# 29 of w_o's 32 blocks summed by row groups in place of 28

## The chip, the core and the metric

The kernel runs on one core of one Trainium2 chip. The metric is the device time of one execution in microseconds, the median over runs. The engines are named as in the profile: PE is TensorE's matmul (PEld its weight loads), DVE VectorE, ACT ScalarE, POOL GpSimd, SP the engine that issues most transfers. Times in a view of the trace are counted from the start of the span, the first instruction of the profiled execution.

## The reference

```python
x = A_x                                   # [2, 1, 512], float32 like everything here
xn = layernorm(x)
q = xn @ wq                               # 32 heads of 128
scores = q . k_cache[last 4096 rows] * 128 ** -0.5     # 8 kv heads, 4 query heads each
o = softmax(scores) . v_cache[last 4096 rows]
s = o.reshape(2, 1, 32 * 128) @ wo        # wo is [4096, 512]
z = gelu(xn @ w_in)                       # [2, 1, 1792]
g = (z1 * (w_sp * layernorm(z2) + b_sp)) @ w_out
out = x + s * silu(g)
```

Some 89 MB are read for two rows of output: 2 x 8 x 4096 x 128 values of each cache, wq (512 x 4096), wo (4096 x 512) and the two weights of the gate.

## The kernel before

Everything large passes through `ring`, four slots of 4 MB in the on-chip memory. `enqueue` and `advance` (lines 85 to 99) hand out the slots in order: SP issues a load as soon as its slots are free. The order of loads is w_in, w_out, wq, then the K and V windows of eight units (one unit is one batch row and two kv heads), and last w_o in three pieces of 16, 8 and 8 blocks.

A block of w_o is a [128, 512] matrix: `wo_v` (line 161) puts row p * 32 + j of w_o in partition p of block j, so s is the sum over 32 blocks of a [128, 2] piece of the attention's output times the block. `load_blocks` (164 to 180) issues one transfer for the first 16 blocks, one for the next 8, and for the last piece `(4, 1, 1, 1, 1)`: one of 1 MB for blocks 24 to 27 and one of 256 KB each for 28, 29, 30 and 31. They come over in that order, and w_o's last block is the last thing that the kernel reads.

Every engine works in program order (`InOrder`, line 27). The loop over units (469 to 497) turns K on DVE, multiplies on TensorE, copies on ACT; 498 to 511 finish the last two units. `collect` (444) multiplies a unit's heads by `sel` into 32 columns of the tile `col`, `gather` (454) makes of that `oT` (line 465), in which `oT[:, n, :]` is block n's left operand: 32 columns of 128 partitions, of which columns 0 and 16 hold the two batch rows.

TensorE's array is used in four column groups of 32 here: a product whose left operand has 32 columns writes 32 rows of the output tile, and four products for different rows (`part[32 * g : 32 * g + 32]`) can run side by side, one in each group. The last projection uses this in two ways.

*By row groups* (516 to 519): block n is multiplied in its full width of 512 columns, into rows of group n % 4 of the tile `part`. Each group sums every fourth block. Afterwards ACT copies `part` to `parts` (521), and `spread_quarters` (310 to 314) multiplies each column quarter of `parts` by `rowm`, which adds the four groups and puts quarter g of the result into rows of group g of the tile `so`. This is called the spread here.

*By column quarters* (523 to 531): block n's 512 columns are cut into four quarters of 128, and quarter g goes straight into rows of group g of `so`, four products per block, with no copy behind them.

`EARLY` is the number of blocks that go by row groups, and the others go by quarters. `LATE` = 30 says ahead of which block of the loop the spread is issued. Before the change: row groups for blocks 0 to 27, ACT's copy, quarters of 28 and 29, the spread, quarters of 30 and 31. All of `so` is one accumulation; DVE then multiplies by the gate (533), adds x (534), and SP stores the result (535).

Every product in this kernel is of float32 values and stands in the trace as two instructions (two passes), each with a weight load of its own.

Of the kernel before, what the change touches and what calls it, by code (L numbers as in the profile page):

```python
# [42 lines left out]
def kernel(  # L43
# [60 lines left out]
    def bank(name, tag):  # L104
        return ps.tile([P, 512], F32, tag=tag, name=name, bufs=BANKS[tag])
# [405 lines left out]
    gather(last)  # L511


    EARLY, LATE = 28, 30
    part = bank("part", "sh")
    for n in range(EARLY):
        t, a = blocks[n]
# [46 lines left out]
```

## Time and profile before

| what | us |
|---|---|
| median of 3 runs (217.80 to 218.05) | 217.91 |
| the profiled execution | 217.37 |
| its span, first to last instruction | 215.6 |
| busy: PE / DVE / ACT | 156.5 / 107.5 / 44.0 |
| HBM read | 89.40 MB, 415 GB/s over the span |
| ACT's copy of `part` | 0.60 |
| products of blocks by row groups, 56 instructions | 7.9 |

The page gives busy time by engine, the span in 40 slices (tenths of each slice, 9 is 90% or more), and the chain of work that ended last, by engine. A row of the timeline has its start and length, the engine, the operation, output and inputs, and a count; like instructions that follow each other are merged, and in brackets stands how long the engine was idle before and what ended that. All rows carry line 37, where the helper `InOrder` issues them, so that one tells instructions apart by their tiles: `part` (row groups), `so` from `ring` (quarters), `so` from `parts` (the spread), `col` (collecting heads). Ends of matmuls are modelled, starts are recorded.

### The profile page before, as it was taken

What the parts mean: (1) busy time and instruction counts of PE and PEld (TensorE: products, weight loads), DVE (VectorE), ACT (ScalarE), POOL (GpSimd) and SP (SyncE); (2) the same over time, 40 slices, a digit from 0 to 9 for tenths busy, and PEclk for the clock granted to TensorE, in tenths of its full rate; (3) what the DMA queues carried; (4) which work ended last, traced back from release to release, by engine and by line L of the source; (5) the groups of instructions that cost most, each with busy time, mean ns of one, the idle gap of its engine ahead of it and who ended that gap; (6) DMA issues with size and microseconds to landing.
All of it is one profiled execution on the core that took longest, in us unless ns stands there. A gap on an engine that the chain in (4) does not pass through costs nothing.

```text
span 215.6 us, 2230 instructions
## 1 busy us (share of the span) xinstructions
PE 156.5 (73%) x866; PEld 43.6 (20%) x866; DVE 107.5 (50%) x168; ACT 44.0 (20%) x109; POOL 3.9 (2%) x21
## 2 busy tenths in 40 slices
PE   0164273952994995995997699559959948999793
PEld 0121110210121221221221222222212212222321
DVE  3304313058968647837906941695587089240101
ACT  5002410000223143133113304120431421232001
POOL 6100000000000000000000000000000000000000
PEclk9999567695598899799699679958997995899799
DMA  7999898999999999999999999999999999999991
GB/s 251 426 528 401 389 499 371 423 444 409 456 407 450 426 435 432 426 438 413 450 412 438 432 438 435 432 432 407 432 444 423 444 426 450 413 441 413 404 388 40
DMA packets 3789, 89.54 MB, mean 415 GB/s; under 512 B 434, under 2 KB 450, under 8 KB 964
## 3 DMA queue, kind: packets, MB, share of 16 engines
q1 hardware_dynamic: 3772, 89.40, 97.0%
q8 instruction: 7, 0.11, 0.2%
q14 instruction: 2, 0.02, 0.0%
q10 hardware_dynamic: 8, 0.00, 0.0%
HBM read 89.40 MB, written 0.00 MB: 415 GB/s over the span
## 4 chain that ended last, share of the span: by engine, by line
DMA 48%; PE 34%; DVE 15%; issue 1%; SPq 0%; DVEq 0%
DMA ring<-in_A_wo_dram 20%; DMA ring<-in_A_wq_dram 16%; DMA ring<-in_A_k_cache_dram 12%; DVE kt L37 10%; PE s L37 10%; PE sh L37 9%; PE acc L37 7%; PE q_ps L37 4%; PE col L37 1%; PE mo L37 1%; DVE qm L37 1%; DVE qbd L37 1%; DVE m L37 1%; PE rp L37 1%; PE oT L37 0%
## 5 line engine op out<-in xcount | busy, mean ns | idle before, releaser
L37 DVE STREAM_TRANSPOSE kt<-ring 128x2048 f32<-128x2048 f32 x32 | 72.6, 2294 | 32.5 <-DMA ring<-in_A_k_cache_dram 30.5
L37 PE MATMUL sh<-kt,qbd 128*32 128x512 f32 x256 | 43.4, 727 | 14.0 <-DVE kt L37 14.0
L37 ACT ACTIVATE shs<-sh 128x512 f32<-128x512 f32 x32 | 19.1, 597 | 119.1 <-PE sh L37 119.1
L37 PE MATMUL s<-shs,add_dq 128*128 128x512 f32 x64 | 41.0, 748 | 0.0
L37 PE MATMUL acc<-ring,pT 128*32 128x512 f32 x256 | 30.3, 612 | 0.2 <-DVE pT L37 0.2
L37 PEld LDWEIGHTS s<-shs,add_dq 128*128 128x128 f32 x64 | 11.2, 219 | 31.1 <-issue 26.7
L37 PEld LDWEIGHTS sh<-kt,qbd 128*32 128x32 f32 x256 | 6.7, 114 | 34.2 <-issue 20.4
L37 PEld LDWEIGHTS acc<-ring,pT 128*32 128x32 f32 x256 | 7.4, 114 | 24.7 <-issue 15.5
L37 PE MATMUL q_ps<-ring,xnT 128*32 128x512 f32 x64 | 9.6, 770 | 3.6 <-DMA ring<-in_A_wq_dram 3.6
L37 PE MATMUL mo<-l,same_r 128*128 128x2 f32 x16 | 3.7, 299 | 10.7 <-ACT p L37 10.7
L37 DVE TENSOR_REDUCE m<-s 128x2 f32<-128x512 f32 x8 | 5.4, 675 | 9.1 <-PE s L37 9.1
L37 ACT ACTIVATE o<-acc,wd 128x128 f32<-128x128 f32 x32 | 9.1, 373 | 3.4 <-PE acc L37 3.4
L37 PE MATMUL z<-ring,xnT 128*32 128x448 f32 x32 | 5.6, 875 | 5.3 <-DMA ring<-in_B_w_in_dram 5.3
L37 ACT ACTIVATE p<-s,nb 128x256 f32<-128x256 f32 x16 | 7.6, 490 | 7.0 <-DVE nb L37 6.8
L37 PE MATMUL part<-ring,oT 128*32 128x512 f32 x56 | 7.9, 714 | 1.1 <-DMA ring<-in_A_wo_dram 1.1
L37 PE MATMUL col<-o,sel 128*32 128x512 f32 x16 | 8.3, 601 | 0.4 <-ACT o L37 0.4
L37 DVE STREAM_TRANSPOSE qT<-q_ps 128x512 f32<-128x512 f32 x2 | 1.4, 717 | 10.4 <-PE q_ps L37 10.2
L37 PE MATMUL y<-ring,hT 128*32 128x512 f32 x14 | 3.5, 1043 | 3.8 <-DVE hT L37 3.8
L37 DVE STREAM_TRANSPOSE pT<-p 128x512 f32<-128x512 f32 x8 | 5.4, 674 | 1.2 <-ACT p L37 1.2
L37 DVE TENSOR_TENSOR res<-so,gate 128x128 f32<-128x128 f32 x1 | 0.3, 292 | 10.8 <-PE so L37 10.8
L37 ACT ACT_TABLE_LOAD x4 | 5.1, 1283 | 1.9 <-issue 1.9
L37 PEld LDWEIGHTS mo<-l,same_r 128*128 128x128 f32 x16 | 3.0, 233 | 12.2 <-ACT p L37 12.2
(106 smaller groups left out, 63.2 us busy)
## 6 DMA issues: line engine op xcount, KB each, us to landing
ring<-in_A_k_cache_dram SPq DMA_DIRECT2D x8, 4096.0 KB, 27.5
ring<-in_A_v_cache_dram SPq DMA_DIRECT2D x8, 4096.0 KB, 30.1
ring<-in_A_wo_dram SPq DMA_DIRECT2D x1, 4096.0 KB, 34.2
ring<-in_B_w_in_dram SPq DMA_DIRECT2D x1, 3584.0 KB, 11.7
ring<-in_A_wo_dram SPq DMA_DIRECT2D x1, 2048.0 KB, 27.5
ring<-in_B_w_out_dram SPq DMA_DIRECT2D x1, 1792.0 KB, 15.5
ring<-in_A_wo_dram SPq DMA_DIRECT2D x1, 1024.0 KB
ring<-in_A_wo_dram SPq DMA_DIRECT2D x4, 256.0 KB, 16.7
```

Source lines behind the costliest of these rows:

```text
L37: return self.tc.keep_in_program_order(call(*args, **kwargs))
```

## The change

One number: `EARLY` goes from 28 to 29. Block 28 moves from the quarters to the row groups.

```diff
-    EARLY, LATE = 28, 30
+    EARLY, LATE = 29, 30
     part = bank("part", "sh")
     for n in range(EARLY):
         t, a = blocks[n]
         g = n % G
         pe.matmul(part[32 * g : 32 * g + 32, :], oT[:, n, :], t[:, a, :], start=(n < G), stop=(n >= EARLY - G))
     parts = sb.tile([P, D], F32, tag="shs", name="parts")
     act.activation(parts, part, AF.Copy)
     so = bank("so", "mo")[:, :DC]
     for n in range(EARLY, 32):
         if n == LATE:
             spread_quarters(so, parts, start=False, stop=False)
...
```

Group 0 of `part` then sums eight blocks (0, 4, ..., 28), the other three groups seven. ACT's copy comes behind block 28's product, and the order on TensorE is: row groups for blocks 0 to 28, quarters of 29, the spread, quarters of 30 and 31. Transfers and their order are unaltered.

## The prediction

> **What bounds the kernel now.** I read the page first, then the chain of waits near the end, then the timeline of the last 14 us, since the diff touches nothing ahead of the last projection.
>
> ```profile
> span 215.6 us, 2230 instructions
> ...
> PE 156.5 (73%) x866; PEld 43.6 (20%) x866; DVE 107.5 (50%) x168; ACT 44.0 (20%) x109; POOL 3.9 (2%) x21
> ...
> DMA  7999898999999999999999999999999999999991
> ...
> DMA 48%; PE 34%; DVE 15%; issue 1%; SPq 0%; DVEq 0%
> ```
>
> The transfers are busy for nine tenths or more of nearly every slice, while the busiest engine has 73%; so the last bytes of w_o arrive at a time that this edit can't move: it changes no transfer. The profiled execution took 217.37 us, of which 1.77 us lie outside the span; the three runs have a median of 217.91 us, 0.54 us more. What is at stake is the stretch behind the last landings. The chain of waits, cut to its end (start, length, what):
>
> ```profile
> 201.94 9.95 DMA ring<-in_A_wo_dram
> 211.89 0.04 issue
> 211.94 0.47 PE so L37 x8
> 212.41 0.02 issue
> 212.43 0.30 DVE res L37
> 212.73 0.02 issue
> 212.76 0.29 DVE res L37
> ```
>
> So block 31's landing at 211.89 sets the end; its eight matmul instructions (four column quarters, and every product of this type runs as two passes), two DVE operations and the store follow. TensorE comes second, and the question is by how much. The timeline of that stretch (start, length, engine, operation, output<-inputs, count; in brackets the idle time before and what ended it):
>
> ```profile
> 209.36 0.16 PEld L37 LDWEIGHTS part<-ring,oT 128*32 128x32 f32 x8 [1.33 <-DMA ring<-in_A_wo_dram]
> 209.36 1.07 PE L37 MATMUL part<-ring,oT 128*32 128x512 f32 x8 [0.42 <-DMA ring<-in_A_wo_dram]
> 210.03 0.34 PEld L37 LDWEIGHTS so<-ring,oT 128*32 128x32 f32 x8 [0.52 <-DMA ring<-in_A_wo_dram]
> 210.25 0.86 PE L37 MATMUL so<-ring,oT 128*32 128x128 f32 x16
> 210.56 0.60 ACT L37 ACTIVATE parts<-part 128x512 f32<-128x512 f32 x1 [12.16 <-PE part L37]
> 210.68 0.16 PEld L37 LDWEIGHTS so<-ring,oT 128*32 128x32 f32 x8 [0.30 <-DMA ring<-in_A_wo_dram]
> 211.20 0.16 PEld L37 LDWEIGHTS so<-parts,rowm 128*32 128x32 f32 x8 [0.37 <-ACT parts L37]
> 211.21 0.43 PE L37 MATMUL so<-parts,rowm 128*32 128x128 f32 x8
> 211.34 0.24 PEld L37 LDWEIGHTS so<-ring,oT 128*32 128x32 f32 x8
> 211.45 0.92 PE L37 MATMUL so<-ring,oT 128*32 128x128 f32 x16
> 211.94 0.16 PEld L37 LDWEIGHTS so<-ring,oT 128*32 128x32 f32 x8 [0.35 <-DMA ring<-in_A_wo_dram]
> ```
>
> The weight loads that waited for a transfer give the landings: blocks 24 to 27 just before 209.36, block 28 before 210.03, 29 before 210.68, 31 before 211.94. Block 30's load, at 211.34, waited for none: it had landed while the spread was being issued. Narrow windows of the same timeline split the merged rows:
>
> ```profile
> 209.82 0.61 PE L37 MATMUL part<-ring,oT 128*32 128x512 f32 x4
> ...
> 210.25 0.40 PE L37 MATMUL so<-ring,oT 128*32 128x128 f32 x8
> ...
> 211.34 0.29 PE L37 MATMUL so<-parts,rowm 128*32 128x128 f32 x4
> ...
> 211.45 0.40 PE L37 MATMUL so<-ring,oT 128*32 128x128 f32 x8
> ...
> 211.94 0.43 PE L37 MATMUL so<-ring,oT 128*32 128x128 f32 x8
> ```
>
> From them come two paces. Four full-width blocks, one in each column group of 32, start their second passes at 209.82 and leave the array to the next operand at 210.25: 0.43 us for a pass of 512 columns. The spread's second pass starts at 211.34 and block 30 follows at 211.45: 0.11 us for a pass of 128. Block 30 therefore occupies the array until 211.45 + 2 x 0.11 = 211.67, and block 31 comes at 211.94: TensorE has 0.27 us to spare, the only cover at the end.
>
> **The change part by part.** In the instruction streams only TensorE's differs: the row-group sum goes from 28 products of 512 columns to 29, the quarter products ahead of the spread from 8 to 4. Loads, queues, ACT, DVE and GpSimd keep theirs in the same order, and no queue of transfers is passed by anything.
>
> Removed: block 28's quarters, eight instructions at 210.25, 2 x 0.11 = 0.22 us of the array. They weren't on the path: the array then idled until block 29 landed (0.30 us of idle load queue before 210.68). Worth nothing.
>
> Added: one product of 512 columns for block 28. It is the 29th, so it goes to column group 0, and no other block goes into groups 1 to 3 beside it. What a lone one costs is shown where the heads are collected, against the four together above:
>
> ```profile
> 198.45 1.04 PE L37 MATMUL col<-o,sel 128*32 128x512 f32 x2 [0.42 <-ACT o L37]
> ```
>
> The same shape alone, two passes: 1.04 us from start to end. Four blocks side by side, eight instructions: 1.07 us. A lone block costs nearly the time of four, and the clock was the same, 1.00 (window, its length, busy time of PE, PEld, DVE, ACT and POOL, granted clock, share of DMA, GB/s):
>
> ```profile
> 197.00:201.70 4.70, 3.15 (x16) 1.21 (x11) 0.89 (x2) 1.14 (x4) 0.00 (x0) 1.00 0.95 405
> 201.80:205.10 3.30, 3.04 (x16) 0.90 (x20) 0.00 (x0) 0.00 (x0) 0.00 (x0) 0.50 1.00 427
> 205.20:215.40 10.20, 6.52 (x84) 2.03 (x76) 0.58 (x2) 0.60 (x1) 0.00 (x0) 1.00 0.53 208
> ```
>  In group 0 the pass before it ends streaming at 210.25; block 28 has landed by 210.03, so its weights load under that pass (0.11 us each by the row below, which gives shortest, median and longest in ns; with no cover a pass takes 1.04 - 0.59 = 0.45, longer by 0.02).
>
> ```profile
> L37 PEld LDWEIGHTS col<-o,sel x16: 106/108/110, 80.5 to 198.5; 128*32 128x32 f32 x16
> L37 PE MATMUL col<-o,sel x16: 590/592/617, 80.5 to 198.9; 128*32 128x512 f32 x16
> ```
>
> Its passes start at 210.25 and 210.68, and the second ends 0.59 later, at 211.27 (to within the rounding of the rows). Up to now the sum ended at 209.82 + 0.61 = 210.43. The sum ends 0.84 later.
>
> On this point the Trainium skill differs a little: TensorE: Matmul & The Clock Gate, section "Measured speedup vs the span model", has four packed products run 3.07 times faster than one after another, not four times. By it, from the 0.86 us that two passes take here, a lone block would cost 0.86 x 3.07 / 4 = 0.66 us (an estimate from that page), and the change in the end would be about +0.34 us. The trace has 1.04 against 1.07 and I go by it.
>
> Moved: ACT's copy of the sum. It started 210.56 - 210.43 = 0.13 behind the sum and will again, at 211.40; with its 0.60 us it ends at 212.00. Nothing is queued behind it on ACT. Behind the wait on TensorE stand, in order, block 29's quarters (free to run at 210.68 + 0.43 = 211.11 and done with the array at 211.33, in TensorE's idle time, so they cost nothing; without that idle 0.22 us), then the spread, then blocks 30 and 31. The spread followed the copy's end, 211.16, by 0.05; it now starts at 212.05. From the spread's start to block 30's is 211.45 - 211.21 = 0.24, from block 30 to block 31 2 x 0.11, and block 31's eight take 0.40 when they follow others without a wait: 212.05 + 0.24 + 0.22 + 0.40 = 212.91. Up to now 211.94 + 0.43 = 212.37.
>
> Sum: +0.84 (late sum) - 0.27 (spare before block 31) - 0.03 (block 31 without a cold start) = +0.54 us. Block 31 has then been on the chip for 0.6 us, and its wait no longer decides. DVE's two operations and the store follow unaltered. The profiled execution comes to 217.37 + 0.54 = 217.91, the median of runs to 217.91 + 0.54 = **218.45 us**.
>
> Bounds of the new terms: the lone block costs at least a quarter of its round, 0.86 / 4 = 0.22, which leaves no more than the 0.27 of cover and so +0.0; at most its two passes at the slowest pace seen, 2 x 0.85 = 1.70 (below), which is 0.84 more than I take. The value comes from the collecting product, since it is the same shape, alone, at the same clock. The spare of 0.27 depends on how far block 31 lands behind blocks 24 to 27 (211.89 - 209.36 here); if that gap is 0.2 us wider or narrower in the median run, the result is +0.34 or +0.74. Nothing is removed from the path, so the bound below is zero.
>
> **The rivals.** (A) Not slower: the column groups share one rate of input, so that a lone product streams up to four times as fast as one among four, and block 28 costs a quarter of a round, 0.22. Then the sum ends 0.22 later, the spread starts at 211.43, and the array is free for block 31 at 211.67 + 0.22 = 211.89, before its weights are there at 211.94: the time stays 217.91. For it: four groups' second passes run in one row of 0.61, and no lone product stands in the tail itself. Against it: the lone collecting product, which took 1.04 for its two passes at the same clock. It holds as long as the sum is less than 0.27 late. Should the freed 0.22 us of quarters count as well, it would be a little faster, for which I see no place.
>
> (B) TensorE is late already in ordinary runs. They take 0.54 us more than the profiled one. If that excess comes from TensorE, it lies ahead of blocks 24 to 27 and has eaten the 0.42 us of idle there and the spare before block 31; TensorE is then 0.42 + 0.27 + 0.54 = 1.23 us later against the landings, the sum's delay has no cover (from 0.69 us on), and the time is 217.91 + 0.84 = 218.75. For it: the clock was halved, 0.50, from 201.80 to 205.10, as the row-group products began. A longer halved stretch would do it: 3.3 us at half pace already costs 1.65. Against it: an excess of the transfers, busy throughout, moves every landing alike and leaves +0.54.
>
> (C) The halved clock reaches the tail. There the passes of four blocks start 0.85 apart:
>
> ```profile
> 202.89 0.22 PEld L37 LDWEIGHTS part<-ring,oT 128*32 128x32 f32 x4 [0.63 <-issue]
> 203.74 0.23 PEld L37 LDWEIGHTS part<-ring,oT 128*32 128x32 f32 x4 [0.63 <-issue]
> 204.59 0.23 PEld L37 LDWEIGHTS part<-ring,oT 128*32 128x32 f32 x4 [0.63 <-issue]
> ```
>
> Block 28 would cost 1.70 in place of 0.86: 218.45 + 0.84 = 219.29. Against it: the clock was 1.00 for all of 205.2 to 215.4. The Trainium skill (the same page, "What's actually happening") says that the gate's window of about 3.4 us runs free, so that its phase may differ from one execution to the next; the profile's 0.50 stretch of 3.3 us agrees with that length, and a shift of phase is why (C) has a chance at all.
>
> That the change doesn't do what it says I exclude: the compiled order has the 29th product in place of four quarters.
>
> **How the numbers follow.** My forecast has 0.70, with a range of its own of 218.25 to 218.65; A 0.12, B 0.13, C 0.05. The range takes in B and the near part of the way to C, and leaves out A's and C's middle, 0.17: 217.95 to 218.90. No change means within 0.2%, 0.44 us, about what a measurement of this kernel can tell: slower begins at 218.35. Of the forecast's 0.70 some 0.15 fall below that (a wider landing gap, or the estimate by the page), so slower has 0.55 + 0.13 + 0.05 = 0.73, same 0.15 + 0.09 of A = 0.24, and the last 0.03 of A is faster.
>
> **What would show it.** In the changed profile: two lone product rows for block 28 starting at 0.43 spacing behind blocks 24 to 27, ahead of any quarter; the copy about 0.84 later against block 27's landing; TensorE's longest wait of the tail for the copy and none for a transfer before block 31; the chain's last releaser the copy instead of the transfer. If block 31's loads still wait for their transfer, the mechanism is A; if the sum ends less than 0.3 us later, the price of a lone block is wrong; if TensorE had no idle time before blocks 24 to 27, B.

## The result, and the profile after

| | runs | median us | lowest to highest |
|---|---|---|---|
| before | 22 | 217.81 | 217.52 to 218.37 |
| after | 22 | 218.57 | 218.12 to 219.36 |

The ratio is 1.0036, with a 95% interval of 1.0026 to 1.0045: slower by 0.36%, some 0.78 us with an interval of 0.57 to 0.98. The forecast was 218.45 us.

The profiled execution of the changed kernel took 218.33 us, with a span of 216.4. Its timeline behind the landing of blocks 24 to 27, columns as before:

```profile
209.65 0.16 PEld L37 LDWEIGHTS part<-ring,oT 128*32 128x32 f32 x8 [1.48 <-DMA ring<-in_A_wo_dram]
209.65 1.47 PE L37 MATMUL part<-ring,oT 128*32 128x512 f32 x9 [0.57 <-DMA ring<-in_A_wo_dram]
210.29 0.35 PEld L37 LDWEIGHTS part<-ring,oT 128*32 128x32 f32 x2 [0.49 <-DMA ring<-in_A_wo_dram]
210.91 0.16 PEld L37 LDWEIGHTS so<-ring,oT 128*32 128x32 f32 x7 [0.27 <-issue]
210.91 0.31 PE L37 MATMUL so<-ring,oT 128*32 128x128 f32 x3
210.96 0.59 PE L37 MATMUL part<-ring,oT 128*32 128x512 f32 x1
211.05 0.72 PE L37 MATMUL so<-ring,oT 128*32 128x128 f32 x5
211.39 0.11 PEld L37 LDWEIGHTS so<-ring,oT 128*32 128x32 f32 x1 [0.32 <-issue]
211.65 0.60 ACT L37 ACTIVATE parts<-part 128x512 f32<-128x512 f32 x1 [13.10 <-PE part L37]
212.30 0.16 PEld L37 LDWEIGHTS so<-parts,rowm 128*32 128x32 f32 x8 [0.80 <-ACT parts L37]
212.30 0.43 PE L37 MATMUL so<-parts,rowm 128*32 128x128 f32 x8 [0.53 <-ACT parts L37]
212.44 0.46 PEld L37 LDWEIGHTS so<-ring,oT 128*32 128x32 f32 x16
212.54 0.62 PE L37 MATMUL so<-ring,oT 128*32 128x128 f32 x16
213.23 0.29 DVE L37 TENSOR_TENSOR res<-so,gate 128x128 f32<-128x128 f32 x1 [11.48 <-PE so L37]
```

Eight passes of blocks 24 to 27 and the first of block 28 make the first row of matmuls; the second pass of block 28 stands alone at 210.96 and ends at 211.55. ACT's copy starts at 211.65. From the start of blocks 24 to 27 to the copy it is now 2.00 us (211.65 - 209.65), where it was 1.20 (210.56 - 209.36); to DVE's first operation 3.58 (213.23 - 209.65), where it was 3.07 (212.43 - 209.36). The tail is 0.51 us longer. The rest of the 0.96 us between the two profiled executions (218.33 - 217.37) lies outside the stretch that the edit touches: blocks 24 to 27 were available 0.29 us later, and 0.16 us more lie outside the span.

In a narrow window of the same timeline block 28's first pass starts at 210.53, so the passes are 0.43 apart:

```profile
210.53 0.59 PE L37 MATMUL part<-ring,oT 128*32 128x512 f32 x1
```

The end of the chain of waits has changed hands:

```profile
193.27 16.33 DMA ring<-in_A_wo_dram
209.60 0.04 issue
209.65 1.47 PE part L37 x9
211.12 0.10 PE so L37 x3
211.22 0.34 PE part L37
...
211.65 0.60 ACT parts L37
212.25 0.04 issue
212.30 0.91 PE so L37 x24
```

The last transfer on the chain is that of blocks 24 to 27, no longer block 31's. Behind it stand the sum with its lone block, the copy, then the spread and blocks 30 and 31 without a gap (24 instructions in 0.91 us). Once blocks 24 to 27 have landed, TensorE's longest idle time, 0.53 us, is for the copy, and none is for a transfer.

### The profile page after: what moved, and what is told of

It is laid out like the page before. It is cut to its first block, busy times and chain, and to the rows that moved or that the text cites. A ratio compares the mean times of both kernels' runs of the same rounds, so it can differ in the third digit from the quotient of the medians.

```text
span 216.4 us, 2218 instructions
## 1 busy us (share of the span) xinstructions
PE 156.8 (72%) x860; PEld 43.5 (20%) x860; DVE 107.5 (50%) x168; ACT 44.0 (20%) x109; POOL 3.9 (2%) x21
## 4 chain that ended last, share of the span: by engine, by line
DMA 47%; PE 32%; DVE 18%; issue 1%; SPq 0%; ACT 0%; DVEq 0%; ACTq 0%
DMA ring<-in_A_k_cache_dram 24%; DMA ring<-in_A_wq_dram 16%; DVE kt L37 13%; PE s L37 9%; PE sh L37 9%; DMA ring<-in_A_wo_dram 8%; PE acc L37 5%; PE q_ps L37 5%; PE mo L37 1%; PE part L37 1%; PE col L37 1%; DVE qm L37 1%; DVE qbd L37 1%; DVE m L37 1%; DVE pT L37 1%
## 5 line engine op out<-in xcount | busy, mean ns | idle before, releaser
L37 PE MATMUL sh<-kt,qbd 128*32 128x512 f32 x256 | 41.8, 709 | 14.9 <-DVE kt L37 14.9
L37 PE MATMUL acc<-ring,pT 128*32 128x512 f32 x256 | 30.8, 619 | 0.2 <-DVE pT L37 0.2
L37 PE MATMUL part<-ring,oT 128*32 128x512 f32 x58 | 8.7, 703 | 1.4 <-DMA ring<-in_A_wo_dram 1.4
```

The costliest lines, as they stand in the source:

```text
L37: return self.tc.keep_in_program_order(call(*args, **kwargs))
```

## The experiments

**A lone product without block 28.** The first two kernels keep 28 blocks by row groups and add one or four products to the sum whose left operand is all zeros.

```diff
+    none = const("none", 32)
+    nc.gpsimd.memset(none, 0.0)
...
+    for g in range(EXTRA):        # EXTRA is 1, then 4
+        pe.matmul(part[32 * g : 32 * g + 32, :], none, t[:, a, :], start=False, stop=True)
```

> The kernel before (28 blocks by row groups) with one more product of 512 columns in column group 0 behind block 27, its left operand all zeros, so that the sum is unaltered. My theory: a lone product costs the whole of its two passes, the sum ends 0.84 us later, and the time is 0.5 to 0.8 us over the kernel before, like the change, though it waits for no further block. Rival A: a quarter of that, within 0.1 us of before. A rival in which block 28's later landing is what costs: also within 0.1 us of before.

> The same with four such products, one in each column group. My theory: they run side by side in the time of one, so this is within 0.1 us of the run with one. Rival A: four cost four times as much as one, about 0.5 us more than the run with one.

One more: 218.54 us, 1.0029 times the kernel before (1.0019 to 1.0040). Four more: 218.43 us, 1.0024 (1.0015 to 1.0034). Both as my theory has it. One product reproduces the change's delay without a wait for any further block (0.73 us by the medians, where the change has 0.76), and four in four groups cost no more than one: 0.11 us less by the medians, where rival A has some 0.5 us more. The timeline of the kernel with one:

```profile
209.69 1.07 PE L37 MATMUL part<-ring,oT 128*32 128x512 f32 x8 [0.27 <-DMA ring<-in_A_wo_dram]
210.58 0.59 PE L37 MATMUL part<-ring,none 128*32 128x512 f32 x1
210.58 0.42 PE L37 MATMUL so<-ring,oT 128*32 128x128 f32 x6
211.01 0.59 PE L37 MATMUL part<-ring,none 128*32 128x512 f32 x1
...
211.70 0.60 ACT L37 ACTIVATE parts<-part 128x512 f32<-128x512 f32 x1 [12.80 <-PE part L37]
```

Its passes start 0.43 apart, like block 28's, and the copy starts 2.01 us behind blocks 24 to 27 (211.70 - 209.69), where the change has 2.00. In the kernel with four, the eight passes of the added round lie in one row of 1.05 us, as long as any full round:

```profile
210.63 1.05 PE L37 MATMUL part<-ring,none 128*32 128x512 f32 x8
```

Rival A falls with this pair.

**The spread behind block 31.** The changed kernel, with what follows the copy reduced to the spread:

```diff
     for n in range(EARLY, 32):
-        if n == LATE:
-            spread_quarters(so, parts, start=False, stop=False)
...
-                start=(n == EARLY), stop=(n == 31),
+                start=(n == EARLY), stop=False,
             )
+    spread_quarters(so, parts, start=False, stop=True)
```

> The changed kernel with the spread issued behind block 31's quarters in place of ahead of block 30's. My theory: the end is set by ACT's copy, and what follows the copy on TensorE is then the spread alone and no longer 16 quarter instructions of blocks 30 and 31 as well (0.44 us); since block 31's own quarters occupy the array until about 0.1 us after the copy has ended, the gain is some 0.35 us: 0.2 to 0.4 us over the kernel before. If the total work on TensorE's queue sets the end and not the copy, the order doesn't matter and it is as slow as the change, 0.6 to 0.9 us over the kernel before.

217.99 us, 1.0010 (1.0001 to 1.0020): 0.18 us over the kernel before by the medians, just better than the 0.2 to 0.4 expected. Three quarters of the change's delay go without any work taken away, so what waits behind the copy is what costs, and not the amount of work on TensorE. It does not get below the kernel before.

**Two kinds of execution.** The granted clock is the share of its full speed that TensorE's clock was let have, and each execution has a mean of it. The changed kernel's executions fall in two groups by this mean, so the kernel before was run again for its own.

> The kernel before once more, for the granted clock of each of its executions. Those of the changed kernel fall in two groups: ten at a mean clock of 0.842 or 0.843 took 218.70 to 219.36 us, twelve at 0.848 to 0.866 took 218.12 to 218.60. If in low-clock executions TensorE is already late ahead of the tail (rival B), the kernel before has two such groups as well, some 0.4 us apart, less than the 0.65 us of the changed kernel, and the change costs about 0.55 us in the one and about 0.84 in the other. If only the transfers differ, its times show no relation to the clock, or the groups lie as far apart as with the change, and the change costs the same in both.

217.76 us for 11 runs. With the 63 runs of the kernel before beside the experiments (its 22 runs beside the change have no clock on record), split at a mean clock of 0.846:

| kernel | above: runs, median us | below: runs, median us |
|---|---|---|
| before | 58, 217.81 | 16, 218.11 |
| after | 12, 218.37 | 10, 219.01 |
| difference | 0.56 | 0.90 |

The groups exist before the change too, 0.30 us apart (some 0.4 was expected) and not 0.64, and the change costs 0.56 us in one and 0.90 in the other, near the forecast's 0.54 and rival B's 0.84. Before the change the groups overlap in time: the 16 executions below run from 217.54 to 218.46, the 58 above from 217.37 to 218.34. By the same split the late spread lies 0.03 us over the kernel before in the upper group (217.84, seven runs) and 0.29 in the lower (218.40, five): where the cover holds, it takes away nearly all of the delay.

What differs is seen in profiles from both groups. That of the kernel with the late spread fell in the lower one (mean clock 0.842), and up to the sum it is the changed kernel. Windows of the changed kernel's profile (0.848), with the columns explained in the prediction:

```profile
201.00:204.40 3.40, 2.60 (x17) 1.08 (x20) 0.21 (x1) 0.00 (x0) 0.00 (x0) 0.62 0.99 419
204.40:207.70 3.30, 3.30 (x32) 0.95 (x28) 0.00 (x0) 0.00 (x0) 0.00 (x0) 0.87 0.96 398
```

and of the one with the late spread, followed by rows of its timeline:

```profile
201.00:204.40 3.40, 1.95 (x12) 0.68 (x16) 0.14 (x1) 0.00 (x0) 0.00 (x0) 0.50 1.01 429
204.40:207.70 3.30, 3.30 (x20) 0.83 (x16) 0.00 (x0) 0.00 (x0) 0.00 (x0) 0.50 0.96 399
```

```profile
202.45 9.20 PE L37 MATMUL part<-ring,oT 128*32 128x512 f32 x57 [1.56 <-DMA ring<-in_A_wo_dram]
...
209.83 0.13 PEld L37 LDWEIGHTS part<-ring,oT 128*32 128x32 f32 x4 [0.35 <-DMA ring<-in_A_wo_dram]
210.20 0.14 PEld L37 LDWEIGHTS part<-ring,oT 128*32 128x32 f32 x4 [0.24 <-issue]
...
212.17 0.60 ACT L37 ACTIVATE parts<-part 128x512 f32<-128x512 f32 x1 [14.23 <-PE part L37]
```

The clock is halved through both windows. TensorE then works without a gap from 202.45 to the last pass of the sum but one, and no longer waits for blocks 24 to 27: their weights are loaded when they land, at 209.83, but their first pass starts only at 210.20, behind the passes of blocks 0 to 23, the first half of them at half pace. The copy starts 2.34 us behind that landing (212.17 - 209.83), not 2.00. That is rival B's mechanism. The two other profiles from the lower group, with four added products (the first row below) and with 24 blocks by row groups (the second, of an experiment further down), have the sum in one row without a gap as well:

```profile
202.12 8.69 PE L37 MATMUL part<-ring,oT 128*32 128x512 f32 x56 [1.45 <-DMA ring<-in_A_wo_dram]
...
202.57 8.01 PE L37 MATMUL part<-ring,oT 128*32 128x512 f32 x48 [1.56 <-DMA ring<-in_A_wo_dram]
```

In the five profiles from the upper group TensorE idles 0.27 to 0.57 us for blocks 24 to 27. Of the kernel before there is no profile from the lower group, so where its 0.30 us come from isn't shown.

**Keeping the clock up.** To test it, three products that nothing reads fill TensorE's idle time ahead of w_o's first block, in the changed kernel and in the one before.

```diff
     scale_out(last)
...
+    keep_busy(256)                # a product of so many columns into a spare bank
     collect(last)
+    keep_busy(512)
     gather(last)
+    keep_busy(512)
```

> The changed kernel with three products of float32 values that nothing reads (256, 512 and 512 columns) in TensorE's idle time between the collecting of the last heads and w_o's first block. Theory B: the executions of the changed kernel near 219.0 us have TensorE's clock halved for 6.8 us in place of 3.4 while it works on w_o's first blocks, so that it comes late to blocks 24 to 27. If these products keep the clock up, that group goes, the times lie within some 0.4 us of each other, the median is 218.2 to 218.4, and 0.55 us over the kernel before remain from the lone product. If the two groups come from the transfers, they stay and the median is about 218.6. If the products delay w_o's first block by more than the clock gives, the median is over 218.7.

> The kernel before with the same three unread products. Theory B: its few executions near 218.1 us go, the others stay as they are, because block 31's landing sets their end: median 217.65 to 217.8, and the difference to the changed kernel with these products is 0.5 to 0.6 us. If the groups come from the transfers: the same as the kernel before in all.

With the change: 218.28 us, 1.0017 times the kernel before (1.0007 to 1.0028). Without it: 217.92, 0.9998 (0.9989 to 1.0007). Windows of the first:

```profile
201.00:204.40 3.40, 3.23 (x26) 1.30 (x29) 0.21 (x1) 0.00 (x0) 0.00 (x0) 1.00 1.00 426
204.40:207.70 3.30, 2.13 (x24) 0.52 (x19) 0.00 (x0) 0.00 (x0) 0.00 (x0) 1.00 0.96 397
```

The halved stretch is gone, and none of the 12 and 11 executions has a mean clock below 0.854. The changed kernel's median fell by 0.29 us, and its slowest execution from 219.36 to 218.74. The kernel before gained nothing in the median: 217.92 is a miss against the 217.65 to 217.8 expected, and only its slowest executions went (218.09 at most in 11 runs, where the 29 runs of the kernel before beside it reach 218.46). In its profile the end still waits for block 31:

```profile
212.31 0.16 PEld L37 LDWEIGHTS so<-ring,oT 128*32 128x32 f32 x8 [0.33 <-DMA ring<-in_A_wo_dram]
```

What agrees less, too: the changed kernel's runs spread over 0.75 us, not 0.4, and the medians of the pair differ by 0.36 us where 0.5 to 0.6 was expected. By the profiles of the pair the tail differs by 0.54:

```profile
209.88 1.48 PE L37 MATMUL part<-ring,oT 128*32 128x512 f32 x9 [0.57 <-DMA ring<-in_A_wo_dram]
...
213.46 0.29 DVE L37 TENSOR_TENSOR res<-so,gate 128x128 f32<-128x128 f32 x1 [11.86 <-PE so L37]
```

with the change, 3.58 us from the one to the other, and without it

```profile
209.76 1.07 PE L37 MATMUL part<-ring,oT 128*32 128x512 f32 x8 [0.57 <-DMA ring<-in_A_wo_dram]
...
212.80 0.29 DVE L37 TENSOR_TENSOR res<-so,gate 128x128 f32<-128x128 f32 x1 [10.78 <-PE so L37]
```

3.04 us. The interval of the first ratio, 0.15 to 0.61 us, holds 0.36 and 0.54 alike, and the runs don't tell whether the difference between them is more than scatter.

**Fewer by row groups, and one more.** `EARLY, LATE` = 24, 26 takes the copy forward; 30, 30 makes two lone products (the spread then starts the accumulation).

> 24 blocks by row groups, the spread ahead of block 26's quarters, blocks 24 to 31 by quarters: no lone product, and the copy runs while TensorE waits for blocks 24 to 27. My theory: where block 31's landing sets the end nothing changes, so within 0.1 us of the kernel before in the median; where TensorE is late the copy's some 0.8 us are no longer on its way, so executions at a lower clock lie at most 0.2 us above the others, not 0.35. If blocks by quarters cost TensorE more than by row groups (8 instructions in place of 2 for each), it is slower than before by 0.2 us or more.

> 30 blocks by row groups: blocks 28 and 29 alone in groups 0 and 1; the spread, which then starts the accumulation of the result, ahead of block 30. My theory: the groups run independently, so block 29's two passes start when it lands, 0.62 us behind block 28, and the sum ends about 0.38 us later than with 29 blocks: 218.85 to 219.05 us. If lone products in different groups run one after another, the sum ends 0.86 us later: about 219.4. If the delay came from the number of products and not from the round that isn't filled, it would be the change's 0.76 us once more: about 219.3.

With 24: 218.20 us (218.16 without one execution of 760 us, which the ratio leaves out too), 1.0007 (0.9996 to 1.0019). Half a miss: above a mean clock of 0.846 its seven executions have a median of 217.93, 0.10 us over the kernel before beside them, as expected, but at a lower clock it isn't better than the kernel before, as its four executions took 218.24 to 218.86, some 0.4 us above the others where at most 0.2 was expected. Its profile is one of these, and in it the sum of 24 blocks itself ends late, so that only two blocks' quarters cover the copy:

```profile
210.38 0.62 PE L37 MATMUL so<-ring,oT 128*32 128x128 f32 x16
210.70 0.60 ACT L37 ACTIVATE parts<-part 128x512 f32<-128x512 f32 x1 [12.64 <-PE part L37]
211.34 0.16 PEld L37 LDWEIGHTS so<-parts,rowm 128*32 128x32 f32 x8 [0.60 <-ACT parts L37]
211.35 0.43 PE L37 MATMUL so<-parts,rowm 128*32 128x128 f32 x8 [0.34 <-ACT parts L37]
211.59 1.49 PE L37 MATMUL so<-ring,oT 128*32 128x128 f32 x48
```

TensorE idles 0.34 us for the copy, and six blocks, 48 instructions, still stand behind it. A spread further back wasn't tried, and whether blocks by quarters cost TensorE more than by row groups, the other case of the expectation, isn't settled.

With 30: 218.87 us, 1.0037 (1.0023 to 1.0051, six runs), within the 218.85 to 219.05 of my theory and far from the 219.3 and 219.4 of the others. The second lone product, in another group, runs beside the first.

```profile
209.45 2.36 PE L37 MATMUL part<-ring,oT 128*32 128x512 f32 x12 [0.56 <-DMA ring<-in_A_wo_dram]
210.12 0.32 PEld L37 LDWEIGHTS part<-ring,oT 128*32 128x32 f32 x2 [0.52 <-DMA ring<-in_A_wo_dram]
210.76 0.14 PEld L37 LDWEIGHTS part<-ring,oT 128*32 128x32 f32 x2 [0.32 <-DMA ring<-in_A_wo_dram]
211.91 0.60 ACT L37 ACTIVATE parts<-part 128x512 f32<-128x512 f32 x1 [13.55 <-PE part L37]
```

Block 29's weights are loaded when it lands, at 210.76, 0.64 us behind block 28's, and the sum ends at 211.81. The copy starts 2.46 us behind blocks 24 to 27, 0.46 later than with 29 (0.38 was expected), and not 0.86. No version was faster than the kernel before.

## Why the prediction was right

*The price of the lone block.* Right: two passes at 0.43 us each, 0.86 in all. A round (here the products that run side by side, at most one in each group) with one product is as long as one with four; the pair of kernels with zeros shows it. The trace's 1.04 against 1.07 was the better guide. The estimate from the Trainium skill (TensorE: Matmul & The Clock Gate, section "Measured speedup vs the span model"), +0.34 us, is outside the measured interval of 0.57 to 0.98; the 3.07 that it starts from is that page's figure for four products packed by rows of the array, and the groups here are columns.

*The copy.* Forecast 0.84 us later against the landing, measured 0.80 in the profile (2.00 - 1.20): the copy followed the lone pass by 0.10 and not by 0.13.

*What stands behind the copy.* Right: the spread, block 30 and block 31 run through without a wait, and block 31's landing no longer counts. Moving the spread behind them took 0.58 us off the median (218.57 - 217.99).

*The sum.* +0.54 forecast, +0.51 in the profiles' tails, +0.56 in the runs at a higher clock. The median is 0.2 us above that since 10 of the 22 executions are at a lower clock, where the cover ahead of blocks 24 to 27 is used up and the change costs 0.90. The term that was mis-sized is the spare time on TensorE: I took it from one execution, 0.27 and 0.42 us, and gave its absence 0.13 as a case of all runs; it is absent in a part of them. Of the 0.64 us between the two groups, 0.30 are in the kernel before as well. That the median still lies in the forecast's own range, 218.25 to 218.65, is luck in part: the lower group begins at 218.70, and with more than half of the executions in it the median would have been outside.

*Rival B.* Its mechanism is real in a part of the executions, but not by the route given there. The 0.54 us by which ordinary runs of the kernel before exceed the profiled one doesn't come from the lower clock in the main: at the higher clock alone they run from 217.37 to 218.34. Where that excess comes from isn't shown.

*Removed quarters.* Worth nothing, as said.

Why the lower clock was more frequent with the change (10 of 22 executions, against 16 of 74 of the kernel before in other sets of runs) stays open.

## What to carry to other kernels

Here a product of 512 columns held its column group for 0.86 us whether the other three groups had work or not. So an item that comes alone costs as much as four side by side: balance the split at multiples of the number of groups, unless the last round is off the path that sets the end. Among 24, 28, 29 and 30 blocks the multiples of four came out best, though 24 and 28 weren't told apart. When a sum has a copy and a second step behind it, count what is queued behind that second step too. And a cover read from one execution is one draw: where the clock's phase differs from one execution to the next, look for the group of executions in which the cover is gone before trusting it.

## What was not expected of the hardware

The program issues products in order, but products in different column groups don't start in that order. In the changed kernel three quarter instructions of block 29, by their number those of the three groups without block 28, start at 210.91, ahead of block 28's second pass at 210.96 that was issued before them. In the kernel with one added product it is plainer: six quarter instructions start from 210.58 on and end by 211.00, ahead of the added product's second pass at 211.01. Starts are recorded; by the modelled ends the order differs too (211.22 against 211.55 in the changed kernel). This differs from the Trainium skill (TensorE: Matmul & The Clock Gate, section "The mechanism"), by which matmuls start and end strictly in order; it cost nothing here, since ACT waits for the pass itself.

Three products in idle time, 2.95 us of busy rows in all (0.70, 1.13 and 1.12 in the changed kernel's timeline with them), removed the halved clock behind them (0.50 for 3.3 us in the kernel before, for 6.7 us in the kernel with the late spread), yet the median fell only where TensorE sets the end.
